# Decode attention over two caches: the last loads reordered to K, K, V, V, V, and the last three PVs placed behind the last scores

## The chip, the cores and the metric

One core of one Trainium2 chip. The metric is the device time of one execution in microseconds (us), as the median of several runs. The profiled execution of a kernel is one of its runs; its span is about 1.8 us shorter than the device time, because the span counts from the first to the last instruction.

## The reference

Two independent blocks, A and B, each with one query token per batch entry against a cache; the outputs are concatenated.

```python
# cut: random inputs, in bfloat16, and the second block, which is the same
B, Sq, D = 8, 1, 1024
H, Sk, Dh = 32, 4096, 128
q = (x @ wq).reshape(B, Sq, H, Dh).transpose(0, 2, 1, 3)
scores = einsum("bhqd,bhkd->bhqk", q, k_cache) * (Dh ** -0.5)
p = softmax(scores)
o = einsum("bhqk,bhkd->bhqd", p, v_cache)
out = o.transpose(0, 2, 1, 3).reshape(B, Sq, H * Dh) @ wo
```

The two K caches and two V caches are read once: 1.07 GB. That is nearly all of the traffic, and there is almost no arithmetic per byte.

## The kernel before

The work is cut into 128 tiles `n`, each of one batch entry and four heads. For each, one K tile and one V tile of 4 MiB are loaded. VectorE multiplies K by the broadcast query (L261), folds the products once (L266), TensorE sums groups with an identity matrix (L274, called "reduce matmuls" below), and VectorE finishes the sum (L280). Each tile is done in four chunks, `s = 4 n + r`. ScalarE then takes the exps (L303), and TensorE multiplies them with V (L316, "PV"). ScalarE copies the result out of PSUM (L322), TensorE extracts the useful blocks (L330), and once per eight tiles the row sums (L337), the normalisation (L344, L345) and the output projection (L356) follow.

All big loads go through one ring of five slots. A tile's place in `order` fixes its slot, and its load is issued when the tile five places earlier is used up:

```python
order = [("k", 0)]
for n in range(NQ):                      # NQ = 128
    if n + 1 < NQ:
        order.append(("k", n + 1))
    order.append(("v", n))
pos = {kn: i for i, kn in enumerate(order)}

def freed(i):
    kind, n = order[i]
    return opEacc.get(NR * n + NR - 1) if kind == "k" else opPV.get((n, NR - 1))
# [cut: load_tiles issues load i once freed(i - NSLOT) exists; the last tile is loaded in four pieces]
```

So it ends K126, V125, K127, V126, V127. The order of the work on each engine is the order in which this loop emits it; in these traces no engine does the work behind an instruction that waits (in loads_only below, TensorE stands still for 5.20 us at one PV and the work behind it waits too):

```python
for s in range(NS + 16):                 # NS = 512 chunks
    n, r = divmod(s, NR)
    # [cut: make_mul(s), make_red(s - 1), make_rmax, make_fold(s), make_ngm, make_exp(n - 1) when r == 0]
    for k in range(2):
        v, w = divmod(s - PL - k, NR)    # PL = 7: PV(v) in chunks 4 v + 7 and 4 v + 8
        if w == 0 and 0 <= v < NQ:
            make_pv(v, 2 * k)
            make_pv(v, 2 * k + 1)
            if k == 1:
                make_acc(v)              # ScalarE copies PV(v) out of PSUM
    # [cut: make_ext(v) one chunk later: extraction, and the row sums after the eighth tile of a block]
    if s < NS:
        make_eacc(s, fold)               # the reduce matmuls
    # [cut: make_norm, make_proj, weight loads]
    load_tiles()
```

PV125 thus belongs to chunks 507 and 508 and PV126 to chunks 511 and 512 (the 512 chunks count from 0, so the second stands behind the last scores). The exps live in `PM`, a ring of 2, and `exp(n)` waits for `PV(n - 2)`.

## Time and profile before

| | before |
|---|---|
| device time, median of the first 3 runs | 2607.15 us (2606.45 to 2608.35) |
| span of the profiled execution | 2605.4 us |
| moved by DMA while it streams | about 430 GB/s |
| VectorE, wait for K in total | 481 us in 125 waits |

These lines of the page of the kernel before are the busy share of the DMA engines in 40 equal slices (9 is 90% or more), the chain of work that ended last, by engine, and the group of VectorE's multiply: busy time and mean ns of one, then its idle time before them and what ended most of it.

```profile
DMA  9999999999999999999999999999999999999996
...
DMA 69%; DVE 22%; PE 6%; ACT 1%; issue 1%; SPq 0%
...
L261 DVE TENSOR_TENSOR ring<-ring,qbc 128x4096 bf16<-128x4096 bf16 x512 | 1165.2, 2276 | 481.4 <-DMA ring<-in_A_k_cache_dram 247.7
```

The slices show a stream that never rests until the last slice. The Trainium skill, page "DMA: Bandwidth & Descriptors", Specifications, gives a fabric ceiling of 435 GB/s; the 430 GB/s of this trace agree with it. The chain says that the end of the kernel is reached by way of DMA for 69% of the span. The group says that VectorE waits for K tile after tile: it is faster than the stream.

A change that takes nothing from the stream can only gain after the last K tiles land. This is the timeline of the kernel before in that stretch. Columns: start and length in us, engine, line, operation, tiles, count, and in brackets the idle time of the engine just before and what ended it.

```profile
2553.10 2.29 DVE L261 TENSOR_TENSOR ring<-ring,qbc 128x4096 bf16<-128x4096 bf16 x1 [3.19 <-DMA ring<-in_B_k_cache_dram]
...
2572.53 2.29 DVE L261 TENSOR_TENSOR ring<-ring,qbc 128x4096 bf16<-128x4096 bf16 x1 [3.19 <-DMA ring<-in_B_k_cache_dram]
...
2586.71 1.88 PE L316 MATMUL pv<-ring,PM 128*16 128x512 bf16 x16
...
2587.56 1.21 DVE L266 TENSOR_TENSOR ring<-ring 128x2048 bf16<-128x2048 bf16 x1
...
2588.83 1.19 PE L274 MATMUL red<-ring,ident 128*128 128x512 bf16 x4 [0.24 <-DVE ring L266]
...
2589.94 1.04 PE L316 MATMUL pv<-ring,PM 128*16 128x512 bf16 x16
...
2593.99 0.60 ACT L322 ACTIVATE accS<-pv 128x512 bf16<-128x512 f32 x1
...
2594.64 0.25 PE L330 MATMUL o<-E,accS 128*128 128x4 bf16 x4 [3.66 <-ACT accS L322]
...
2594.83 2.50 PE L316 MATMUL pv<-ring,PM 128*16 128x512 bf16 x32
...
2598.16 1.85 PE L337 MATMUL o<-rsum,mask 128*128 128x8 f32 x8
...
2600.68 1.87 PE L356 MATMUL proj<-WO,on_sb 128*8 128x512 bf16 x8 [0.68 <-DVE on_sb L345]
```

VectorE starts on K126 at 2553.10 and, four chunks later, would be free at 2569.34. It stands still for 3.19 us until K127 lands. Its last fold ends at 2588.77 (2587.56 + 1.21), and 16.63 us follow to the end of the span: the last reduce matmuls, the last exps on ScalarE (ending at 2593.97), PV127, copy, extraction, row sums, projection, store. The second halves of PV125 and PV126 stand in these stages without holding anything up.

TensorE runs at two clocks. The same view in fixed stretches shows its busy time (and the number of matmuls), the granted clock, the DMA share and GB/s:

```profile
2588.00:2591.00 3.00, 2.75 (x28) 0.81 0.13 52
2591.00:2594.00 3.00, 0.00 (x0) 1.00 0.01 5
2594.00:2600.00 6.00, 4.66 (x48) 0.67 0.00 0
```

Sixteen matmuls of a PV took 1.04 us at clock 1.00 (at 2589.94) and 1.88 us at 0.50 (at 2586.71). The tail has a mixture of both.

### The profile page before, as it was taken

To read this page: it belongs to the slowest core of one execution; us is meant where nothing else is said; L and a number is where in the kernel's file an instruction comes from. 1 tells how busy PE (TensorE), PEld (TensorE's weight loads), DVE (VectorE), ACT (ScalarE), POOL (GpSimd) and SP (SyncE) were. 2 spreads that over 40 slices of the span, in tenths; PEclk is the share of its full clock that TensorE was granted. 3 is DMA by queue.
4 is the path that set the end of the run, shared out by engine and by line. 5 is a ranking of instruction groups with operands and counts; after the bars stand their busy time and mean duration, and the time that the engine had idled before them with its cause. 6 is when DMAs were issued, how large, how long until landed. Compare 5 with 4: busy or idle time off the path is not lost.

```text
span 2605.4 us, 18877 instructions
## 1 busy us (share of the span) xinstructions
PE 1384.3 (53%) x7568; PEld 384.2 (15%) x7568; DVE 2085.8 (80%) x1833; ACT 445.6 (17%) x1427; POOL 3.2 (0%) x15
## 2 busy tenths in 40 slices
PE   4455554555545555455554564545545455455545
PEld 1111111111111111111111111111111111111111
DVE  7778887888878878788787887878878787888786
ACT  1112111121112111121111211211112111121111
POOL 0000000000000000000000000000000000000000
PEclk8666665766666666666666666666666666666666
DMA  9999999999999999999999999999999999999996
GB/s 409 427 430 431 431 426 430 430 429 431 426 431 430 431 429 428 430 431 429 430 426 429 433 428 432 428 428 431 430 430 422 428 433 428 432 431 431 430 429 295
DMA packets 54247, 1108.58 MB, mean 425 GB/s; under 512 B 4576, under 2 KB 4608, under 8 KB 21008
## 3 DMA queue, kind: packets, MB, share of 16 engines
q1 hardware_dynamic: 54160, 1107.38, 99.4%
q8 instruction: 59, 0.97, 0.2%
q14 instruction: 28, 0.23, 0.0%
HBM read 1107.33 MB, written 0.03 MB: 425 GB/s over the span
## 4 chain that ended last, share of the span: by engine, by line
DMA 69%; DVE 22%; PE 6%; ACT 1%; issue 1%; SPq 0%
DMA ring<-in_B_k_cache_dram 32%; DMA ring<-in_A_k_cache_dram 30%; DVE ring L261 12%; DVE ring L266 7%; DMA ring<-in_A_v_cache_dram 4%; PE red L274 3%; DVE s_sb L280 3%; DMA ring<-in_B_v_cache_dram 3%; PE pv L316 2%; ACT PM L303 1%; PE o L337 1%; DVE rmax L286 0%; PE proj L356 0%; PE misc L232 0%; ACT accS L322 0%
## 5 line engine op out<-in xcount | busy, mean ns | idle before, releaser
L261 DVE TENSOR_TENSOR ring<-ring,qbc 128x4096 bf16<-128x4096 bf16 x512 | 1165.2, 2276 | 481.4 <-DMA ring<-in_A_k_cache_dram 247.7
L274 PE MATMUL red<-ring,ident 128*128 128x512 bf16 x2048 | 887.1, 583 | 989.4 <-DVE ring L266 989.4
L266 DVE TENSOR_TENSOR ring<-ring 128x2048 bf16<-128x2048 bf16 x512 | 621.1, 1213 | 0.0
L274 PEld LDWEIGHTS red<-ring,ident 128*128 128x128 bf16 x2048 | 213.9, 126 | 1456.3 <-DVE ring L266 1198.7
L316 PE MATMUL pv<-ring,PM 128*16 128x512 bf16 x4096 | 397.7, 504 | 7.2 <-DMA ring<-in_A_v_cache_dram 4.6
L280 DVE TENSOR_REDUCE s_sb<-red 128x32 f32<-128x512 f32 x512 | 349.2, 682 | 16.0 <-PE red L274 16.0
L296 ACT ACTIVATE bias<-ngm 128x1 f32<-128x1 f32 x128 | 26.0, 203 | 1593.5 <-DVE ngm L290 1593.4
L303 ACT ACTIVATE PM<-s_sb,bias 32x128 bf16<-32x128 f32 x512 | 294.9, 576 | 15.2
L330 PE MATMUL o<-E,accS 128*128 128x4 bf16 x512 | 34.0, 171 | 211.1 <-ACT accS L322 211.1
L316 PEld LDWEIGHTS pv<-ring,PM 128*16 128x16 bf16 x4096 | 99.1, 101 | 283.5 <-issue 238.3
L303 ACT ACTIVATION_READ_ACCUMULATOR PM<-s_sb,bias 32x1 f32 x512 | 128.1, 250 | 0.0
L251 ACT ACTIVATE qbc<-misc 128x128 bf16<-128x128 f32 x128 | 35.5, 278 | 385.6 <-PE misc L246 385.6
L322 ACT ACTIVATE accS<-pv 128x512 bf16<-128x512 f32 x128 | 76.5, 597 | 6.3 <-PE pv L316 2.8
L330 PEld LDWEIGHTS o<-E,accS 128*128 128x128 bf16 x512 | 23.4, 106 | 320.1 <-ACT accS L322 320.1
L286 DVE TENSOR_REDUCE rmax<-s_sb 128x1 f32<-128x128 f32 x128 | 36.6, 286 | 4.4
L246 PE MATMUL misc<-q_sb,selb 8*32 8x128 bf16 x512 | 37.3, 282 | 0.8 <-ACT q_sb L237 0.8
L232 PE MATMUL misc<-WQ,xT 128*8 128x512 bf16 x128 | 33.6, 410 | 6.4 <-DMA WQ<-in_A_wq_dram 6.4
L237 ACT ACTIVATE q_sb<-misc 8x512 bf16<-8x512 f32 x16 | 9.4, 587 | 143.8 <-PE misc L232 143.8
L337 PE MATMUL o<-rsum,mask 128*128 128x8 f32 x128 | 29.7, 361 | 0.0
L246 PEld LDWEIGHTS misc<-q_sb,selb 8*32 8x32 bf16 x512 | 13.4, 96 | 106.8 <-issue 106.8
L337 PEld LDWEIGHTS o<-rsum,mask 128*128 128x128 f32 x128 | 28.5, 328 | 0.0
L290 DVE TRANSPOSE_TENSOR_REDUCE ngm<-rmax 128x1 f32<-128x32 f32 x128 | 26.1, 204 | 0.0
(25 smaller groups left out, 59.0 us busy)
## 6 DMA issues: line engine op xcount, KB each, us to landing
ring<-in_A_k_cache_dram SPq DMA_DIRECT2D x64, 4096.0 KB, 39.8
ring<-in_A_v_cache_dram SPq DMA_DIRECT2D x64, 4096.0 KB, 31.5
ring<-in_B_k_cache_dram SPq DMA_DIRECT2D x64, 4096.0 KB, 40.7
ring<-in_B_v_cache_dram SPq DMA_DIRECT2D x63, 4096.0 KB, 32.1
WQ<-in_A_wq_dram SPq DMA_DIRECT2D x4, 2048.0 KB, 40.8
WO<-in_A_wo_dram SPq DMA_DIRECT2D x8, 1024.0 KB, 37.6
WQ<-in_B_wq_dram SPq DMA_DIRECT2D x4, 2048.0 KB, 44.4
WO<-in_B_wo_dram SPq DMA_DIRECT2D x8, 1024.0 KB, 37.7
```

Source lines behind the costliest of these rows:

```text
L246: i = e.matmul(misc[MP * j:MP * (j + 1), 0:Dh], selb[:, b, :], q_sb[:, blk % 4, j * Dh:(j + 1) * Dh], start=True, stop=True, tile_position ...
L251: "act", lambda e: e.activation(qbc[:, n % 2, :], misc[:, 0:Dh], ACTF.Copy),
L261: opMul[s] = add("dve", lambda e: e.tensor_tensor(v, v, qbc[:, n % 2, :].unsqueeze(1).to_broadcast([128, CT, Dh]), ALU.mult), [opT[("k", n ...
L266: return add("dve", lambda e: e.tensor_tensor(v[:, :, 0:64], v[:, :, 0:64], v[:, :, 64:128], ALU.add), [opMul[s]])
L274: i = e.matmul(dst, ident[:], v[:, :, j, :], start=(j == 0), stop=(j == 3))
L280: opRed[s] = add("dve", lambda e: e.tensor_reduce(s_sb[:, n % 3, r * CT:(r + 1) * CT], red_ps[s % 2][:, :].rearrange("p (t w) -> p t w", w ...
L286: opRmax[n] = add("dve", lambda e: e.tensor_reduce(rmax[:, n % 2:n % 2 + 1], s_sb[:, n % 3, :], AX.X, ALU.max), [opRed[NR * n + NR - 1]])
L303: return e.activation(PM[rows, n % 2, :, j], s_sb[rows, n % 3, :], ACTF.Exp, bias=bias[rows, n % 2:n % 2 + 1], scale=scale, accum_out=rsum ...
L316: i = e.matmul(bank[32 * q:32 * q + 4 * HQ, :], PM[:, n % 2, t:t + 4, :].rearrange("p t j -> p (t j)"), v[:, t * Dh:(t + 4) * Dh], start=( ...
L322: opAcc[n] = add("act", lambda e: e.activation(accS[:, n % 2, :], pv_ps[n % 2][:], ACTF.Copy), [opPV[(n, NR - 1)], _at(opExt, n - 2)])
L330: x = e.matmul(o_ps[blk % 2][:, HQ * b:HQ * (b + 1)], accS[:, n % 2, i * 128:(i + 1) * 128], E16[:, i, :], start=(i == 0), stop=(i == 3))
L337: x = e.matmul(o_ps[blk % 2][:, 64 + B * j:64 + B * (j + 1)], mask[:, j:j + 1].to_broadcast([128, 128]), rsum[:, blk % 2, :], start=True, ...
```

## The change

The intent: load K127 one place earlier, so that VectorE need not wait for it, and let V125 come after it. V125 is then late for its old place in TensorE's order. So the last three PVs move behind the last scores, and a third set of exps has to be kept.

```diff
-        PM = sb("PM", [128, 2, T, HQ], BF16)
+        PM = sb("PM", [128, 3, T, HQ], BF16)
...
-        for n in range(NQ):
-            if n + 1 < NQ:
-                order.append(("k", n + 1))
-            order.append(("v", n))
+        for n in range(NQ - 3):
+            order += [("k", n + 1), ("v", n)]
+        order += [("k", NQ - 2), ("k", NQ - 1), ("v", NQ - 3), ("v", NQ - 2), ("v", NQ - 1)]
...
-    ... PM[rows, n % 2, :, j] ...  _at(opPV, (n - 2, NR - 1))
+    ... PM[rows, n % 3, :, j] ...  _at(opPV, (n - 3, NR - 1))
...
+        pv_at = {max(NR * v + PL, NS + 2 * (v - NQ + 3) if v >= NQ - 3 else 0): v for v in range(NQ)}
...
-                v, w = divmod(s - PL - k, NR)
-                if w == 0 and 0 <= v < NQ:
+                v = pv_at.get(s - k)
+                if v is not None:
# [cut: the same replacement for extraction, normalisation, projection and weight loads;
#  the counting of DMA semaphores is moved into add(), with the same counts]
```

Only the last two swap places in the queue: `order` now ends K126, K127, V125, V126, V127. PV125, PV126 and PV127 stand in chunks 512 and 513, 514 and 515, 516 and 517.

More of the change, by code (lines that the diff above doesn't have):

```diff
@@ L39, in __init__ @@
         self.ops = {e: [] for e in ENGINES}
+        self.counts = {}
     def add(self, eng, emit, deps=(), dma_key=None):
         op = _Op(eng, emit, list(deps), dma_key)
+        if dma_key is not None:
+            self.counts[dma_key] = self.counts.get(dma_key, 0) + 16
+            op.token = (dma_key, self.counts[dma_key])
         for d in op.deps:
@@ L49, in tokens @@
     def tokens(self):
-        counts = {}
+        counts = self.counts
         for e in ENGINES:
             for op in self.ops[e]:
-                if op.dma_key is not None:
-                    counts[op.dma_key] = counts.get(op.dma_key, 0) + 16
-                    op.token = (op.dma_key, counts[op.dma_key])
-                elif op.sig:
+                if op.dma_key is None and op.sig:
                     counts[e] = counts.get(e, 0) + 1
@@ L302, in emit @@
                 def emit(e, j=j, rows=rows):
-                    return e.activation(PM[rows, n % 2, :, j], s_sb[rows, n % 3, :], ACTF.Exp, bias=bias[rows, n % 2:n % 2 + 1],
+                    return e.activation(PM[rows, n % 3, :, j], s_sb[rows, n % 3, :], ACTF.Exp, bias=bias[rows, n % 2:n % 2 + 1],
                                         scale=scale, accum_out=rsum[rows, blk % 2, b:b + 1])
-                opExp[n].append(add("act", emit, [opBias[n], _at(opPV, (n - 2, NR - 1)), _at(opLsum, blk - 2), c_PM]))
+                opExp[n].append(add("act", emit, [opBias[n], _at(opPV, (n - 3, NR - 1)), _at(opLsum, blk - 2), c_PM]))
         def make_pv(n, r):
@@ L315, in emit @@
                         t = 4 * (4 * g + q)
-                        i = e.matmul(bank[32 * q:32 * q + 4 * HQ, :], PM[:, n % 2, t:t + 4, :].rearrange("p t j -> p (t j)"),
+                        i = e.matmul(bank[32 * q:32 * q + 4 * HQ, :], PM[:, n % 3, t:t + 4, :].rearrange("p t j -> p (t j)"),
                                      v[:, t * Dh:(t + 4) * Dh], start=(g == 0), stop=(g == RG - 1), tile_position=(0, 32 * q))
@@ L404, in _build_kernel @@
                         make_acc(v)
-            v, w = divmod(s - PL - 2, NR)
-            if w == 0 and 0 <= v < NQ:
+            v = pv_at.get(s - 2)
+            if v is not None:
                 make_ext(v)
@@ L411, in _build_kernel @@
                 make_eacc(s, fold)
-            v, w = divmod(s - PL - 3, NR)
-            if w == 0 and v >= 0 and v % B == B - 1 and v < NQ:
+            v = pv_at.get(s - 3)
+            if v is not None and v % B == B - 1:
                 make_norm(v // B)
-            v, w = divmod(s - PL - 4, NR)
-            if w == 0 and v >= 0 and v % B == B - 1 and v < NQ:
+            v = pv_at.get(s - 4)
+            if v is not None and v % B == B - 1:
                 make_proj(v // B)
-            v, w = divmod(s - PL - 8, NR)
-            if w == 0 and v >= 0 and v % B == B - 1 and v // B + 1 < NB:
+            v = pv_at.get(s - 8)
+            if v is not None and v % B == B - 1 and v // B + 1 < NB:
                 load_wo(v // B + 1)
```

## The prediction

> **What bounds the kernel now.** The DMA stream. In the page's slices the 16 DMA engines are 90% or more busy in 39 of 40 slices at about 430 GB/s; the Trainium skill, page "DMA: Bandwidth & Descriptors", Specifications, gives 435 GB/s as the fabric ceiling, and this trace agrees. One K and one V tile pass every 19.44 us; VectorE works 16.2 us of it and waits 3.2 us for K (chain: 69% DMA; wait table: 481 us on K in 125 waits). The change takes nothing from this stream.
>
> **What is movable: the tail** (timeline). K126 starts on VectorE at 2553.10 and is done at 2569.34. VectorE idles 3.19 us until K127 lands (2572.53) and works to 2588.78 (last fold); 16.6 us follow: reduce matmuls, reduction, maximum, four exps (ending 2593.97), PV127 2.5, copy 0.60, extraction and row sums 2.0, normalisation 0.6, projection 1.9, output 2.8.
>
> **What the change does.**
> 1. K127 takes V125's place in the queue, one tile (estimate 9.7 us) earlier, and lands near 2562.8, before VectorE wants it. The 3.19 us wait disappears; the last fold ends near 2585.6. Issue instants stay: both places are freed by the same work as before.
> 2. PV125 and PV126, which ran on an otherwise idle TensorE, now stand after the last reduce matmuls, in front of PV127. A half PV (16 matmuls) took 1.04 us at clock 1.0 and 1.88 at 0.5. Part hides under the 4 us from last reduce matmul to last exp. But the copy of PV125 stands behind the exps on ScalarE, its extraction waits for it in TensorE's order, and half of PV126 and PV127 come behind that. Estimated cost 0.9 to 2 us.
> 3. The clock. Without PVs TensorE has 1.9 of each 3.9 us busy in the K127 stage, so it should be at 0.5 when the burst starts (last reduce matmuls 1.9 us, not 1.2: +0.7) and reach 1.0 some 3 to 6 us later. The Trainium skill, "TensorE: Matmul & The Clock Gate", Part 1, says that the default is the halved clock and sustained activity over a window of about 3.4 us releases it; the granted clock in this trace flips only at multiples of 3.4 us, between 0.50 and 1.00. The burst may keep the projection at full clock (1.0, not 1.87 us: -0.8).
> 4. Ring of 3 for the exps only lets PV be late. No exp waited for a PV in the waits, so no steady gain. The bigger zeroing (0.95 us, estimate 1.4) lies under the first load. The rewritten semaphore counting counts the same.
>
> Sum: -3.2 (wait) +0.7 (cold reduce) +0.9 to +2 (PVs in the tail) -0.8 (warm projection) gives -1.5 to -3.5, the parts overlapping; I take -2.5. Floor: V127's last bytes land near 2592 and PV127's last quarter is due near 2594.5, so DMA shouldn't bind it.
>
> **Predicted: 2604.7 us, 80% range 2601.5 to 2608.0.** Faster by over 2%: 0.01; within 2%: 0.985; slower: 0.005.
>
> **What the profile would show.** Right: no VectorE wait before K127's first multiply; last fold 3.2 us earlier; PV125 straight after the last reduce matmuls; TensorE idle before the extraction of 125, ended by ScalarE; all before K126 unchanged. Wrong: K127 still awaited; PV127 waiting for V127; half clock through all three PVs (gain near 0).
>
> **What would make it wrong.** Run-to-run movement of the stream (before spans 1.9 us, as large as the effect); the phase of the clock windows; a slow DMA engine that delays K127 or V127: engines finish the last big tiles up to 7 us apart.

## The result, and the profile after

| | before | after |
|---|---|---|
| device time, median of 6 runs each | 2607.14 us (2605.49 to 2608.76) | 2603.76 us (2603.38 to 2604.32) |
| ratio | | 0.9987, 95% interval 0.9974 to 1.0000 |
| span of the profiled execution | 2605.4 us | 2602.3 us |

A ratio is the mean time of one kernel's runs over that of the other's of the same rounds, so it is not quite the ratio of the medians. By the 2% measure the kernels are the same, and the interval just touches 1. But no run overlaps: the changed kernel ran 16 times in all, on three sets of runs, between 2603.21 and 2604.32 us, and the fastest run of the kernel before took 2605.28. The 3.4 us are small and real.

These are the page's lines of the kernel after that answer to those of before:

```profile
DMA  9999999999999999999999999999999999999997
...
DMA 70%; DVE 22%; PE 7%; ACT 1%; issue 1%; SPq 0%
...
L262 DVE TENSOR_TENSOR ring<-ring,qbc 128x4096 bf16<-128x4096 bf16 x512 | 1165.9, 2277 | 476.0 <-DMA ring<-in_A_k_cache_dram 247.4
```

The stream is the same. VectorE's idle time before the multiplies fell from 481.4 to 476.0 us; 3.2 us of that is the wait at the very end; the other 2.2 us lie elsewhere in the stream and moved nothing that follows, for K126 was started at 2553.01 in place of 2553.10.

The timeline of the kernel after (its lines have moved by one: L262 is the multiply, L275 the reduce matmuls, L317 the PVs, L323 the copies, L331 the extractions, L338 the row sums, L357 the projection):

```profile
2553.01 2.29 DVE L262 TENSOR_TENSOR ring<-ring,qbc 128x4096 bf16<-128x4096 bf16 x1 [3.19 <-DMA ring<-in_B_k_cache_dram]
...
2569.18 2.28 DVE L262 TENSOR_TENSOR ring<-ring,qbc 128x4096 bf16<-128x4096 bf16 x1
...
2584.19 1.22 DVE L267 TENSOR_TENSOR ring<-ring 128x2048 bf16<-128x2048 bf16 x1
...
2585.47 1.89 PE L275 MATMUL red<-ring,ident 128*128 128x512 bf16 x4 [2.05 <-DVE ring L267]
...
2587.29 4.67 PE L317 MATMUL pv<-ring,PM 128*16 128x512 bf16 x48
...
2591.37 0.60 ACT L323 ACTIVATE accS<-pv 128x512 bf16<-128x512 f32 x1
...
2592.02 0.25 PE L331 MATMUL o<-E,accS 128*128 128x4 bf16 x4
...
2592.20 1.90 PE L317 MATMUL pv<-ring,PM 128*16 128x512 bf16 x32
...
2594.22 1.04 PE L317 MATMUL pv<-ring,PM 128*16 128x512 bf16 x16
...
2596.08 1.04 PE L338 MATMUL o<-rsum,mask 128*128 128x8 f32 x8
...
2597.79 1.68 PE L357 MATMUL proj<-WO,on_sb 128*8 128x512 bf16 x8 [0.67 <-DVE on_sb L346]
```

The first multiply of K127 starts at 2569.18 with no idle time before it. The last fold ends at 2585.41 (2584.19 + 1.22), 3.36 us earlier than in before. The three PVs stand in a row behind the last reduce matmuls. And the clock:

```profile
2588.00:2591.00 3.00, 3.00 (x32) 0.50 0.11 44
2591.00:2594.00 3.00, 2.94 (x52) 0.97 0.03 8
2594.00:2600.00 6.00, 4.09 (x44) 0.84 0.00 0
```

The ledger of the profiled runs, worked out from the two timelines:

| stretch | before | after | difference |
|---|---|---|---|
| until the end of the last fold | 2588.77 | 2585.41 | -3.36 |
| last fold to end of PV127 | 8.56 | 9.85 | +1.29 |
| end of PV127 to end of span | 8.07 | 7.04 | -1.03 |
| span | 2605.4 | 2602.3 | -3.1 |

### The profile page after: what moved, and what is told of

The parts are those of the page before. It is cut to its first block, busy times and chain, and to the rows that moved or that the text cites. A ratio compares the mean times of both kernels' runs of the same rounds, so it can differ in the third digit from the quotient of the medians.

```text
span 2602.3 us, 18878 instructions
## 1 busy us (share of the span) xinstructions
PE 1383.7 (53%) x7568; PEld 384.3 (15%) x7568; DVE 2086.1 (80%) x1833; ACT 445.7 (17%) x1427; POOL 3.6 (0%) x15
## 4 chain that ended last, share of the span: by engine, by line
DMA 70%; DVE 22%; PE 7%; ACT 1%; issue 1%; SPq 0%
DMA ring<-in_B_k_cache_dram 31%; DMA ring<-in_A_k_cache_dram 30%; DVE ring L262 12%; DVE ring L267 6%; DMA ring<-in_A_v_cache_dram 4%; DMA ring<-in_B_v_cache_dram 4%; PE red L275 3%; DVE s_sb L281 3%; PE pv L317 2%; ACT PM L304 1%; PE proj L357 1%; PE o L338 0%; PE misc L233 0%; DVE rmax L287 0%; ACT accS L323 0%
## 5 line engine op out<-in xcount | busy, mean ns | idle before, releaser
L262 DVE TENSOR_TENSOR ring<-ring,qbc 128x4096 bf16<-128x4096 bf16 x512 | 1165.9, 2277 | 476.0 <-DMA ring<-in_A_k_cache_dram 247.4
L275 PE MATMUL red<-ring,ident 128*128 128x512 bf16 x2048 | 887.2, 583 | 992.2 <-DVE ring L267 992.2
L275 PEld LDWEIGHTS red<-ring,ident 128*128 128x128 bf16 x2048 | 214.3, 127 | 1461.9 <-DVE ring L267 1204.1
L317 PE MATMUL pv<-ring,PM 128*16 128x512 bf16 x4096 | 398.7, 505 | 7.1 <-DMA ring<-in_A_v_cache_dram 4.5
L304 ACT ACTIVATE PM<-s_sb,bias 32x128 bf16<-32x128 f32 x512 | 295.0, 576 | 15.1
L331 PE MATMUL o<-E,accS 128*128 128x4 bf16 x512 | 34.1, 171 | 206.0 <-ACT accS L323 205.9
L317 PEld LDWEIGHTS pv<-ring,PM 128*16 128x16 bf16 x4096 | 99.6, 101 | 282.1 <-issue 236.8
L323 ACT ACTIVATE accS<-pv 128x512 bf16<-128x512 f32 x128 | 76.4, 597 | 6.2 <-PE pv L317 2.8
L331 PEld LDWEIGHTS o<-E,accS 128*128 128x128 bf16 x512 | 23.5, 107 | 314.2 <-ACT accS L323 314.2
L338 PE MATMUL o<-rsum,mask 128*128 128x8 f32 x128 | 28.9, 354 | 0.0
L338 PEld LDWEIGHTS o<-rsum,mask 128*128 128x128 f32 x128 | 27.7, 319 | 0.0
```

What stands on the lines that cost most here:

```text
L262: opMul[s] = add("dve", lambda e: e.tensor_tensor(v, v, qbc[:, n % 2, :].unsqueeze(1).to_broadcast([128, CT, Dh]), ALU.mult), [opT[("k", n ...
L275: i = e.matmul(dst, ident[:], v[:, :, j, :], start=(j == 0), stop=(j == 3))
L304: return e.activation(PM[rows, n % 3, :, j], s_sb[rows, n % 3, :], ACTF.Exp, bias=bias[rows, n % 2:n % 2 + 1], scale=scale, accum_out=rsum ...
L317: i = e.matmul(bank[32 * q:32 * q + 4 * HQ, :], PM[:, n % 3, t:t + 4, :].rearrange("p t j -> p (t j)"), v[:, t * Dh:(t + 4) * Dh], start=( ...
L323: opAcc[n] = add("act", lambda e: e.activation(accS[:, n % 2, :], pv_ps[n % 2][:], ACTF.Copy), [opPV[(n, NR - 1)], _at(opExt, n - 2)])
L331: x = e.matmul(o_ps[blk % 2][:, HQ * b:HQ * (b + 1)], accS[:, n % 2, i * 128:(i + 1) * 128], E16[:, i, :], start=(i == 0), stop=(i == 3))
```

## The experiments

Each kernel ran with timed rounds against the kernel before on the same chip, and all gave correct outputs. Medians are of 5 runs each (9 of the kernel before). "Behind the last fold" is the span's end less the end of VectorE's last fold in the profiled run: it leaves out when the stream happened to deliver. It is worked out in each case from the run's timeline.

| label | median us | before, same chip | ratio (95%) | last fold ends | behind it |
|---|---|---|---|---|---|
| after_again | 2603.31 | 2607.04 | 0.9986 (0.9974 to 0.9999) | 2585.28 | 16.6 |
| loads_only | 2607.34 | 2607.04 | 1.0004 (0.9991 to 1.0016) | 2590.48 | 15.1 |
| late_pv_only | 2606.69 | 2607.04 | 0.9999 (0.9986 to 1.0011) | 2588.69 | 17.1 |
| ring3_only | 2607.20 | 2607.04 | 1.0002 (0.9988 to 1.0015) | 2588.73 | 16.6 |
| warm_pe | 2602.64 | 2607.06 | 0.9984 (0.9972 to 0.9997) | 2585.42 | 15.4 |
| mid_pv | 2604.67 | 2607.06 | 0.9988 (0.9974 to 1.0002) | 2585.41 | 17.6 |
| mid_pv_sums | 2603.09 | 2607.06 | 0.9984 (0.9972 to 0.9997) | 2585.58 | 16.9 |
| after_third | 2603.47 | 2608.47 | 0.9984 (0.9970 to 0.9998) | 2585.08 | 17.0 |
| warm_pe_again | 2604.31 | 2608.47 | 0.9986 (0.9974 to 0.9999) | 2585.69 | 16.2 |
| mid_warm | 2601.49 | 2608.47 | 0.9976 (0.9964 to 0.9989) | 2585.40 | 14.5 |
| mid_sums_warm | 2600.82 | 2608.47 | 0.9973 (0.9961 to 0.9986) | 2585.47 | 13.5 |
| before_warm | 2605.43 | 2606.93 | 0.9993 (0.9980 to 1.0007) | 2588.51 | 14.2 |

The theory: the gain is VectorE's 3.2 us wait for K127, which the load order removes; the PVs have to move out of its way, and the move itself gives nothing. Its rivals: the load order alone gives the gain; or the gain comes from the row of PVs, which ends at full clock; or from the freer ring of exps; or it is only movement of the stream.

### after_again: does it repeat?

No edit.

> The changed kernel as it is, beside before on this chip. Every theory: 3 to 3.5 us below before in the timed runs (2603.8 against 2607.1 so far). If the gain were only movement of the stream from run to run, it would not repeat, and the difference would fall within 1 us.

Measured 3.7 us below before by the medians. It repeats. That it is movement of the stream is out.

### loads_only: the load order without the PV move

```diff
 (against the changed kernel)
-        pv_at = {max(NR * v + PL, NS + 2 * (v - NQ + 3) if v >= NQ - 3 else 0): v for v in range(NQ)}
+        pv_at = {NR * v + PL: v for v in range(NQ)}
```

> Only the load order (and the ring of 3); the PVs stay at their old places, so PV125 stands in TensorE's order in K126's last chunk, before V125 has landed. Theory (the gain is the 3.2 us VectorE wait for K127, and it can be had only if no PV blocks the queue): K127's first multiply starts at once, but TensorE waits 3 to 5 us for V125 in front of reduce matmuls, VectorE then waits for the reduction by about 3 us, and the last fold stays within 1 us of before (2588.8). Total 0 to 1.5 us below before. Rival (the load order alone is the gain, the PV move is only tidying): last fold 3 us earlier, total 3 us or more below before, up to 5.

The gain is gone (2607.34 against 2607.04). From this kernel's timeline, the start of K127's first multiply, the first half of PV125 on TensorE, and VectorE's next reduction:

```profile
2569.41 2.28 DVE L262 TENSOR_TENSOR ring<-ring,qbc 128x4096 bf16<-128x4096 bf16 x1
...
2572.70 1.88 PE L317 MATMUL pv<-ring,PM 128*16 128x512 bf16 x16 [5.20 <-DMA ring<-in_B_v_cache_dram]
...
2576.44 0.69 DVE L281 TENSOR_REDUCE s_sb<-red 128x32 f32<-128x512 f32 x1 [4.75 <-PE red L275]
```

VectorE gets to K127 at once, at 2569.41. But PV125 keeps its old place in TensorE's order, waits 5.20 us for V125, and holds up the reduce matmuls behind it; VectorE then waits 4.75 us for the reduction. The last fold ended 1.7 us later than in before. I had expected it within 1 us; the total of 0.3 us above before lies just outside the 0 to 1.5 us below that I gave, so the block cost somewhat more than I thought. The total even hides part of it: what lies behind the last fold took 15.1 us in place of 16.6 in this profiled run, for PV127 (1.90 us) and the row sums (1.04) happened to run at full clock. The rival that the load order alone is the gain is out. The move of PV125 is what makes the order usable.

### late_pv_only: the PV move without the load order

```diff
 (against the changed kernel)
-        for n in range(NQ - 3):
-            order += [("k", n + 1), ("v", n)]
-        order += [("k", NQ - 2), ("k", NQ - 1), ("v", NQ - 3), ("v", NQ - 2), ("v", NQ - 1)]
+        for n in range(NQ):
+            if n + 1 < NQ:
+                order.append(("k", n + 1))
+            order.append(("v", n))
```

> Old load order, PVs after the last scores, ring of 3. Theory: the wait for K127 of 3.2 us is back, last fold near 2588.7, and the tail behind the last fold is as long as in the changed kernel (16.9 us, against 16.6 in before): total within 1 us of before. Rival (the gain is the TensorE burst that ends at full clock, making row sums 1.04 in place of 1.85 and the projection shorter): tail shorter than before by 1 us or more, total 1 us or more below before.

Its first multiply of K127, from the timeline:

```profile
2572.45 2.29 DVE L263 TENSOR_TENSOR ring<-ring,qbc 128x4096 bf16<-128x4096 bf16 x1 [3.19 <-DMA ring<-in_B_k_cache_dram]
```

The 3.19 us wait is back, and the total is 0.35 us below before, within the noise. What lies behind the last fold is 17.1 us long, a little longer than in before and not shorter. So the PV move gives nothing by itself, as the theory said, and the two parts of the change work only together.

### ring3_only: the ring of 3 and the counting

```diff
 (both edits above together: old load order, old PV places)
```

> Only the ring of 3 and the semaphore counting; old load order and PV places. Theory: no exp waited for a PV in before, so this is before: within 1 us. Rival (freer exps help throughout): 1 us or more below before, with the difference spread over the whole run rather than in the tail.

2607.20 against 2607.04. The ring has no effect of its own that these runs resolve.

### warm_pe and warm_pe_again: TensorE kept busy before the row of PVs

```diff
 (against the changed kernel)
+        def make_warm():                 # 6 matmuls of 128x512 into a bank that is done with
+            ...
             if s < NS:
                 make_eacc(s, fold)
+                if s in (NS - 3, NS - 2):
+                    make_warm()
```

> The changed kernel with 6 extra 128x512 matmuls into an unused bank after each of the reduce groups 509 and 510, to keep TensorE busy before the last reduce matmuls. Tests the clock term: if the half clock at the start of the burst costs what I think, the granted clock reaches 1.0 before the last reduce matmuls (1.04 us in place of 1.89) and the three PVs run at full clock; the last PV then ends 1 to 1.5 us earlier after the last fold, so 0.8 to 2 us below the changed kernel. If the burst's start is hidden under the exps and ScalarE's copies, only the 0.85 us of the reduce group or less comes out. If the extra work delays the reduce matmuls themselves, the last fold moves later by up to 1 us and there is no gain.

> The kernel with 12 extra matmuls before the last reduce group again, now beside the changed kernel on one chip. Clock theory: 0.7 to 1.5 us below the changed kernel, as between chips so far (2602.6 against 2603.3). If that was a difference of chips, none.

In both profiled runs the clock was at 1.00 before the last reduce matmuls, which took 1.04 us in place of 1.89, and the three half PVs behind them 2.77 us in place of 4.67. Most of what that saves turns into a wait: TensorE then stands still in front of the extraction of PV125, for ScalarE's copy, which stands behind the exps.

```profile
2586.43 2.77 PE L324 MATMUL pv<-ring,PM 128*16 128x512 bf16 x48
...
2591.15 0.25 PE L338 MATMUL o<-E,accS 128*128 128x4 bf16 x4 [1.95 <-ACT accS L330]
...
2591.33 1.90 PE L324 MATMUL pv<-ring,PM 128*16 128x512 bf16 x32
```

PV127 ended 0.9 us sooner behind the last fold than in the profiled run of the changed kernel. But the timed runs are inconclusive: 0.7 us below the changed kernel when each is taken from its own chip, and 0.8 us above it (2604.31 against 2603.47) when both ran on one chip. In the second profiled run the extra matmuls, still at half clock, pushed the last reduce group but one back by about 0.3 us, and the projection fell back to half clock (1.87 us). So this crude way of keeping the clock up isn't a reliable gain. Why the timed runs of the second set were slower than the changed kernel's stays open. The two profiled runs of this one kernel already differ: the clock rose at 2580.9 in the first and at 2583.5 in the second. Each trace shows one run, and the steps of the clock lie differently in each.

### mid_pv: PV125 inside K127's stage

With the new load order, V125 is there early in K127's stage (loads_only shows it landed by 2572.70). So PV125 need not go behind the last scores: two chunks later than its old place is enough, and PV126 and PV127 can stay.

```diff
 (against the changed kernel)
-        pv_at = {max(NR * v + PL, NS + 2 * (v - NQ + 3) if v >= NQ - 3 else 0): v for v in range(NQ)}
+        pv_at = {NR * v + PL + (2 if v == NQ - 3 else 0): v for v in range(NQ)}
```

> The new load order with PV125 two chunks later than in before (in the second and third chunk of K127, when V125 has landed) and PV126 and PV127 at their old places. Theory (the wait for K127 was the gain, and the late PVs gave part of it back): last fold as early as in the changed kernel (near 2585.5), one PV and a half less behind it, last PV done near 2593 in place of 2595.3, total 1.5 to 3 us below the changed kernel and 5 to 6 below before. Rival (V127's landing near 2591.5 to 2592 already bounds the tail): at most 0.5 us below the changed kernel, with PV127 waiting for V127.

It missed: 2604.67, not 2600.5 to 2602.3. The last fold was as early as expected. V127 was not awaited, so the rival is wrong too. The total lies 0.9 to 1.4 us above the three medians of the changed kernel, which ran on other chips, in place of 1.5 to 3 below. The ratios to before (0.9988 against 0.9984 to 0.9987) don't separate the two kernels; the gain that I expected isn't there. What happened is in the timeline of TensorE and in its clock, in the columns as before:

```profile
2586.44 1.87 PE L317 MATMUL pv<-ring,PM 128*16 128x512 bf16 x16
2591.14 0.27 PE L331 MATMUL o<-E,accS 128*128 128x4 bf16 x4 [2.83 <-ACT accS L323]
2591.34 3.59 PE L317 MATMUL pv<-ring,PM 128*16 128x512 bf16 x32
...
2595.76 1.85 PE L338 MATMUL o<-rsum,mask 128*128 128x8 f32 x8
2598.29 1.87 PE L357 MATMUL proj<-WO,on_sb 128*8 128x512 bf16 x8 [0.67 <-DVE on_sb L346]
```

```profile
2584.00:2588.00 4.00, 2.52 (x20) 0.81 0.55 225
2588.00:2591.00 3.00, 0.31 (x4) 0.50 0.11 44
2591.00:2594.00 3.00, 2.86 (x32) 0.50 0.01 5
...
2583.10:2586.51 3.41, 1.67 (x24) 1.00 0.58 243
```

TensorE now has nothing to do while ScalarE makes the last exps (2.83 us idle before the extraction), and the granted clock is 0.50 from 2586.5 to the end of the span. In this run the clock fell before that idle stretch, which began at 2588.3: the last line shows the 3.41 us up to the fall, in which TensorE was busy for 1.67 us. So the idle stretch didn't bring the clock down here, as the expectation of mid_warm below has it; at most it kept it down. PV127's 32 matmuls take 3.59 us where 32 of them take 1.90 in the changed kernel, the row sums 1.85 in place of 1.04, the projection 1.87.

### mid_pv_sums: row sums ahead of PV127

```diff
 (against mid_pv)
-            if b == B - 1:
+            if b == B - 1 and n < NQ - 1:
-                ... the 8 matmuls of the row sums ...
+                make_lsum(n)             # the same 8 matmuls, now a function
...
+            if s == NS + 1:
+                make_lsum(NQ - 1)        # ahead of the extraction of 126 and of PV127
```

> As mid_pv, with the row sums of the last block (8 matmuls, 1.04 or 1.85 us) before PV127 instead of behind its extraction, since they need only the exps. Theory: they fill TensorE's wait for V127 and leave the chain: 0.5 to 1.5 us below mid_pv. If TensorE has no idle time there, PV127 starts later by as much and nothing is won.

1.6 us below mid_pv by the medians (2603.09 against 2604.67); that is a little more than I expected. The runs of the two overlap, though (2602.04 to 2604.29 against 2603.22 to 2605.03), and the profiled runs differ by 0.5 us. In its profiled run PV127 again took 3.59 us at half clock. Here the clock stayed at 1.00 until 2590.7, and fell after an idle stretch of TensorE of 3.04 us, which ScalarE's exps ended.

### mid_warm and mid_sums_warm: the idle stretch filled

If the clock ate the gain of mid_pv, then more work for TensorE, in the idle stretch and ahead of the last reduce matmuls, must bring it back, though it computes nothing.

```diff
 (against mid_pv, and against mid_pv_sums)
+            if s == NS + 1:
+                make_warm(12)            # behind PV126, while ScalarE makes the exps
...
+            if s == NS - 1:
+                make_warm(5)             # ahead of the last reduce matmuls
             if s < NS:
                 make_eacc(s, fold)
```

after_third is the changed kernel again, run on the same chip.

> The changed kernel again, on the same chip as the next three, which are to be read against it: 2603 to 2604.

> The kernel with PV125 and PV126 inside K127's stage, plus 5 extra matmuls before the last reduce group and 12 behind PV126, in the stretch of 3 us in which TensorE waited for the exps. Clock theory (that stretch, idle, dropped the clock to 0.50, and half-clock PV127 3.59 us, row sums 1.85 and projection 1.87 ate the gain): the clock stays at 1.00, PV127 takes 1.9, row sums 1.04, projection 1.04, so 2.5 to 3.3 us below the profiled run without the extra matmuls (2604.7), near 2601.5 to 2602. Rival (PV127 was slow because V127's bytes or ScalarE held it back): PV127 stays near 3.6 us and the total near 2604.5.

> The same with the row sums moved ahead of PV127 and all kept at full clock: PV127 begins after the row sums, near 2591.7, and nothing but the copy, extraction, normalisation and projection follow: 0.5 to 1 us below the kernel without the move, so 2600.5 to 2601.5. If TensorE's order makes PV127 start later by all of the row sums' 1.04 us, no gain.

The PV127, row sums and projection of mid_warm, and then its clock:

```profile
2591.31 1.90 PE L324 MATMUL pv<-ring,PM 128*16 128x512 bf16 x32
...
2594.03 1.04 PE L345 MATMUL o<-rsum,mask 128*128 128x8 f32 x8
...
2595.75 1.33 PE L364 MATMUL proj<-WO,on_sb 128*8 128x512 bf16 x8 [0.68 <-DVE on_sb L353]
```

```profile
2588.00:2591.00 3.00, 2.15 (x10) 1.00 0.12 49
2591.00:2594.00 3.00, 2.17 (x39) 1.00 0.01 3
2594.00:2600.00 6.00, 2.40 (x20) 0.70 0.01 3
```

Seventeen matmuls that compute nothing make the program faster: PV127 takes 1.90 us, the row sums 1.04, and the total falls to 2601.49, 3.2 us below mid_pv (other chip) and 2.0 below the changed kernel on the same chip. Every run of mid_warm (at most 2602.15) lies below every run of mid_pv (at least 2603.22). Nothing but the 17 matmuls and the chip differs (mid_pv wasn't run again on this one), and the trace shows the clock at 1.00 where it had been 0.50, so that the clock had eaten the gain of mid_pv is shown. Which of the two places counts isn't: the 5 matmuls fill the stretch before the fall of mid_pv, the 12 the idle one behind it. With the row sums moved too, 2600.82 us: its five runs lie between 2600.72 and 2600.95, 2.65 us below the changed kernel on the same chip. By the medians it is 7.6 us below before on this chip. But before's runs fall into two groups in every set (here 2605.3 to 2607.0 and 2608.5 to 2608.8; why is open), and here its median lies in the upper one, so the ratio of 0.9973 (about 7 us) is the better figure. mid_sums_warm beats both kernels.

### before_warm: the clock alone

```diff
 (against the kernel before: no new load order, no moved PV)
+            if s == NS + 1:
+                make_warm(12)
```

> The kernel before with nothing but 12 extra matmuls behind PV126, in the 3.6 us in which TensorE waits for the last exps. Clock theory, without any change of load order: PV127 1.9 in place of 2.5 us, row sums 1.04 in place of 1.85, projection 1.0 to 1.9 in place of 1.87, so 1 to 2.2 us below before, with VectorE's wait for K127 and the last fold where they were. If the half clock had mattered only in the kernels with moved PVs, no gain.

1.5 us below before by the medians; the interval of the ratio includes 1, though all five runs (at most 2605.56) lie below all nine of before on this chip (at least 2606.06). In the profiled run VectorE waited 3.20 us for K127 as in before, the clock stayed at 1.00 from before the last fold's end until the projection was done, and 14.2 us lay behind the last fold in place of 16.6. So the trace shows a gain of 2.4 us in the tail and the timed runs support some 1.5 of it, without settling it at 95%.

## Why the prediction was right, point by point

The prediction of 2604.7 us (range 2601.5 to 2608.0) held: 2603.76. Its steps:

1. **K127 lands before it is wanted, and the 3.19 us wait goes.** Right. The last fold ended 3.36 us earlier. loads_only and late_pv_only show that this is the gain, and that it needs both parts. K127 landed where it was foreseen, near 2562.8: its load was issued at 2529.70 and took 33.0 us, so it landed at 2562.7 (in before 42.6 us from 2529.92, so 2572.5).
2. **Cold reduce matmuls, +0.7 us.** Right: 1.19 us became 1.89.
3. **Late PVs, +0.9 to +2 us.** Too large. The stretch to the end of PV127 grew by 1.29, of which 0.70 are the reduce matmuls, so the PVs cost 0.59. I had foreseen that they would hide under the exps, but not how well: with PV125 at half clock and the first half of PV126 at full, these three half PVs ended at 2591.96, and the copy that the next instruction waits for ended at 2591.97.
4. **TensorE idle in front of the extraction of 125, ended by ScalarE.** Wrong for the kernel after, for the same reason: 0.06 us. warm_pe shows that idle time, 1.95 us, where the PVs run at full clock.
5. **Projection at full clock, -0.8 us.** Wrong in size: 1.87 us became 1.68, -0.19. But the row sums, which I had counted as fixed, went from 1.85 to 1.04, -0.81. The two together are the -1.0 of the ledger. Their weight loads started 213 ns apart in before and 112 ns apart after, so they went with the granted clock too. That the foreseen -0.8 came out near the measured -1.0 is luck: most of it came from a term that the sum didn't have, and the clock fell again at 2598.0, in the middle of the projection.
6. **Half clock through all three PVs would leave a gain near 0.** This was not put to the test as stated. The clock rose at 2591.2, 5.7 us after the last reduce matmuls began (3 to 6 were foreseen): PV125 ran at half clock, PV126 and PV127 at full. A longer half clock is what mid_pv had, with a smaller gain.
7. **The ring of 3 and the counting do nothing.** Right, by ring3_only.
8. **V127's landing doesn't bind.** Right: PV127 waited for no DMA in any of the variants. It is close, though: V127's last piece landed at 2592.04 in mid_warm, 0.57 us before PV127's last quarter began at 2592.61, so a tail that is shorter still would meet it.

The errors of 3 and 5 go opposite ways. With the measured sizes the sum is -3.2 + 0.7 + 0.6 - 0.8 - 0.2 = -2.9; the profiled runs differ by 3.1 and the medians by 3.4. The term that was mis-sized most is the PVs in the tail.

## What to carry to other kernels

In a kernel that streams, look at the last two or three tiles: which load does the last chain of work wait for, and can that load go ahead of one that has slack? A new load order is worth only as much as the in-order queues behind it allow: here the reordered loads gained nothing until the consumer of the delayed tile moved too. And when work is moved off TensorE, look at the granted clock of what stays: in mid_pv TensorE had so little to do that the whole tail ran at half clock, which cost more than the moved work had, and 17 matmuls that compute nothing won it back.

## What the Trainium skill lacked or had wrong

- "TensorE: Matmul & The Clock Gate", Part 1 and the table "Why this matters for your kernels": the default of half clock and the window of about 3.4 us agree with this trace (stretches of granted clock of 6.83, 13.65 and 17.07 us, 2, 4 and 5 times 3.413). But the table's rule, no idle gaps over about 3 us, is not enough by itself (Part 1, "A second HAM failure mode", tells of frequent short idles that throttle too, without a figure): in mid_pv the clock fell from 1.00 to 0.50 at 2586.5, and in the 3.41 us before that no gap of TensorE was longer than 1.74 us; it was busy for 1.67 us of them. In mid_pv_sums a window with 1.68 us busy did not make it fall, nor did one with 1.51 us in warm_pe (2587.69 to 2591.10), so where the limit lies, and whether it is one of busy time, isn't known from here.
- The same page, section "LDWEIGHTS (loading the stationary operand)", gives one formula, columns over 1.2 in ns (an estimate of 107 ns for 128), without the type or the clock; the section after it excepts FP32 from the fast weight load. The loads of the float32 weights of the row sums, 128 columns, started 213 ns apart at granted clock 0.50 (before) and 112 ns apart at 1.00 (after); their records are 333 and 190 ns long, for one overlaps the next. Only the full clock comes near the formula.
- The same page speaks of warm-up matmuls for benchmarks, not of filler inside a kernel. Here 17 matmuls that compute nothing took mid_pv's 17.6 us behind the last fold to 14.5 us.
- "DMA: Bandwidth & Descriptors", Specifications, gives both 435 GB/s for the fabric and about 358 GB/s for HBM per core, and the section "Where 436 GB/s comes from" says that the second binds between HBM and SBUF. With one core running, the stream held about 430 GB/s until its last slice, so it didn't bind here. The page's section "Measured" agrees with the trace and not with that sentence: its figures, up to 425 GB/s, are for one core with the other core of the pair idle.
